# 2-byte in place of 4-byte TensorE transposes, no dummy matmuls among the first scale columns, and another place for the wait before the last store, in a transformer block

## The chip, the cores and the metric

The kernel runs on one core of a Trainium2 chip. The metric is the device time of one execution in microseconds (us), the median of the runs of a measurement. The core has a matrix engine (TensorE, PE in the profile, its weight loads PEld), VectorE (DVE), ScalarE (ACT) and GpSimd (POOL). SyncE (SP) issues most of the data transfers. All five work from queues of their own and meet through semaphores.

## What is computed

The block has two token sequences of 256 tokens, 1152 features, two heads of 576 and a hidden layer of 4608. All inputs are bf16.

```python
mod = (_silu(c) @ w_mod).reshape(B, 6, 1, D)
shift_a, scale_a, gate_a, shift_m, scale_m, gate_m = [mod[:, i] for i in range(6)]
h = _layernorm(x, axis=-1) * (1 + scale_a) + shift_a
qkv = (h @ wqkv).reshape(B, N, 3, H, Dh)
attn = _softmax(jnp.einsum('bqhd,bkhd->bhqk', q, k) * Dh ** (-0.5), axis=-1)
a = jnp.einsum('bhqk,bkhd->bqhd', attn, v).reshape(B, N, D) @ wo
x = x + gate_a * a
h2 = _layernorm(x, axis=-1) * (1 + scale_m) + shift_m
m = _gelu(h2 @ w_fc1) @ w_fc2
return x + gate_m * m
```

## The kernel before

**Tiles.** The 512 tokens stand in four tiles of 128 partitions (tile t, sequence b = t // 2). Matmuls contract over features, so activations must stand with features on the partitions: 1152 features are 9 slices of 128 (index kt). LayerNorm 1, the softmax and LayerNorm 2 have tokens on the partitions, and their outputs are transposed by TensorE into PSUM, from where VectorE and ScalarE copy them out. PSUM has 8 banks of 2 KB per partition.

**Order of work.** The program is recorded as units (`S.unit`, `S.op`). `Sched.schedule` is a planner: TensorE's and SP's units keep the order in which they are recorded, the other engines take the ready unit with the longest remaining chain, by costs written in the code (a transpose unit costs its count times `c_mm(128)`). For the first part of VectorE's and ScalarE's work the order is written out by hand in `S.first` (lines 935 to 941). `Sched.emit` turns the dependences into semaphore waits. The dependences in PSUM are by whole banks (lines 257 to 279): a read of a bank by ScalarE waits for earlier recorded reads of the same bank by VectorE, and the other way round, and a TensorE write waits for all readers of the bank before it.

**4-byte transposes.** `tr4` (line 703) looks at 256 neighbouring bf16 values of a token as 128 words of 4 bytes and transposes the words against a 4-byte identity (`IDENT4W`, made by GpSimd, line 735). The result has two features in one word: on partition p the features 2p and 2p+1 of the group lie side by side. A LayerNorm tile needs one 2-byte transpose (`tr`, line 707; slice 0) and four of `tr4` (slices 1 to 8, in pairs). So whatever reads the result steps by two elements, and the weight rows that meet it are loaded in the same paired order (`pair`, `wqkv_row`, `fcols`, `wqkv_h`, `wfc1_h`). The softmax transposes have two `tr4` for each of four (sequence, head) pairs, and their pairs are keys, so the value matmuls take every second token (`v0`, line 985).

**The first part.** Fourteen dummy matmuls (`warm(14, "b")`) stand ahead of the first transposes. Then come transposes xnT_1, xnT_0 and the first scale columns (`mod_kt`, units sca_0 to sca_8, 5 matmuls of 2 columns each) in three groups of three kt, as their weights arrive. Two dummy matmuls of 512 columns stand after sca_5 (`warm(2, "c")`), two after sca_8 (`warm(2, "d")`). Then `sc1a`, the scaled slices `hk(kt, b)` for kt 0 to 4 out of PSUM (kt 2 and 4 of sequence 0 and kt 2 of sequence 1 by ScalarE), and the key matmuls, slice by slice; xnT_2 stands after kt 1 and xnT_3 after kt 2. `XB` (line 780) has the three banks of each sequence: slice 0 in the third, slices 1 to 4 in the first, 5 to 8 in the second. `xn_T_copy` copies 5 to 8 out in one ScalarE instruction.

**LayerNorm 2.** `wo_tile(t)` has three chunks of nine matmuls, each followed by VectorE (line 1065) and GpSimd (line 1066), then the statistics and `xn2_t` (ScalarE, line 1071). `xn2_T(t)` has the transposes: slice 0 and slices 5 to 8 in bank 6, 1 to 4 in bank 7. VectorE copies out slices 0 to 3 for tiles 0 and 1 and 0 to 5 for tiles 2 and 3 (line 1088), ScalarE the rest (line 1091). xn2T_0 stands ahead of `wo_tile(3)`, xn2T_1 ahead of its third chunk, xn2T_2 after fc1 tile 3, xn2T_3 after fc1 tile 5 (F0 is 8).

**The end.** The second MLP matmul stores 14 pieces; token tile 3 ends in pieces of 384, 384, 224, 96 and 64 columns. Each piece is multiplied and added on VectorE (lines 1181, 1182) and stored by SP. Before SP issues the last store, lines 469 to 471 wait for the end of all the others.

Of the kernel before, what the change touches and what calls it, by code (L numbers as in the profile page):

```python
# [171 lines left out]
class Sched:  # L172
# [225 lines left out]
    def emit(self, nc, block, sems, dma_sems):  # L398
# [67 lines left out]
        def run_engine(e, eng_handle):  # L466
            for u in order[e]:
                for ins in u.instrs:
                    if ins is last_out:
                        for o in outs[:-1]:  # L470
                            eng_handle.wait_ge(dma_sems[o.dma_sem], o.dma_val)
# [10 lines left out]
            if e == "sp":  # L482
                eng_handle.wait_ge(dma_sems[last_out.dma_sem], last_out.dma_val)
# [11 lines left out]
F32R = mybir.dt.float32r  # L495
# [48 lines left out]
def build_kernel(nc, x, c, wqkv, wo, w_mod, w_fc1, w_fc2, out):  # L544
# [5 lines left out]
    with (  # L550
# [4 lines left out]
        arena_off = nc.sbuf_base - ARENA_BYTES  # L555
        words = nc.alloc_sbuf_tensor_at("words", [P, ARENA_BYTES // 4], F32R, offset=arena_off)

        def sb(off, nbytes, dt=BF16):
            assert off % 4 == 0 and off + nbytes <= ARENA_BYTES, (off, nbytes)
            v = arena[:, off // 2:(off + nbytes) // 2]  # L560
            if dt != BF16:
                v = v.bitcast(dt)
            return v
# [65 lines left out]
        o_id4 = misc(512)  # L629
        IDENT4 = sb(o_id4, 512)  # L630
        IDENT4W = nc.alloc_sbuf_tensor_at("ident4", [P, P], F32R, offset=arena_off + o_id4)[:, :]
# [26 lines left out]
        wqkv_h = wqkv[P:D, :].rearrange("(g p i) f -> p g i f", p=P, i=2)  # L658
        wmod_v = w_mod.rearrange("(k p) f -> p k f", p=P)
        wo_v = wo.rearrange("(k p) f -> p k f", p=P)  # L660
        wfc1_h = w_fc1[P:D, :].rearrange("(g p i) f -> p g i f", p=P, i=2)
# [6 lines left out]

        def pair(kt):
            return (kt - 1) // 2, (kt - 1) % 2  # L670

        def wqkv_row(kt, c0):
            if kt == 0:
                return wqkv[0:P, c0:c0 + D]
            g, i = pair(kt)
            return wqkv_h[:, g, i, c0:c0 + D]

        def fcols(ft):
            if ft == 0:
                return slice(0, P)  # L680
            g, i = pair(ft)
            c0 = P + 256 * g + i
            return slice(c0, c0 + 255, 2)
# [19 lines left out]
        def tr4(o, i_):  # L703
            o4, w0 = o.bitcast(F32R), int(i_.offset) % (ARENA_BYTES // 2) // 2
            S.instr(lambda e: e.transpose(o4, words[:, w0:w0 + P], IDENT4W), reads=[i_, IDENT4], writes=[o])  # L705

# [7 lines left out]
        for (ka, kb) in ((0, KC), (KC, KT)):  # L714
# [4 lines left out]
            for kt in range(ka, kb):  # L719
                dma(WK[:, kt, :], wqkv_row(kt, D), P * D * 2, "ld_wk%d" % kt, run=2304)  # L720
# [3 lines left out]
        def wfc1_load(q):  # L724
            w = WFC1[q % 4]
            dma(w[:, 0, :], w_fc1[0:P, q * 512:(q + 1) * 512], P * 512 * 2, "ld_wfc1_%d_0" % q, run=1024)
            for i in range(2):
                dma(w[:, 1 + i:KT:2, :], wfc1_h[:, :, i, q * 512:(q + 1) * 512], 4 * P * 512 * 2, "ld_wfc1_%d_%d" % (q, 1 + i), run=1024)
# [6 lines left out]
        pool(300, lambda e: e.tensor_copy(IDENT4W, IDENT), [IDENT], [IDENT4], "ident4")  # L735
# [46 lines left out]
        def xn_T(t):  # L782
            b = t // 2
            S.unit("pe", 5 * c_mm(128), "xnT_%d" % t)
            tr(ps16(XB[b][2], (t % 2) * 128, 128), XN[:, t, 0:P], IDENT)
            for g in range(4):
                tr4(ps32(XB[b][g // 2], (g % 2) * 256 + (t % 2) * 128, 128), XN[:, t, P + 256 * g:P + 256 * (g + 1)])

        def xn_src(b, kt):
            if kt == 0:  # L790
                return ps16(XB[b][2], 0, 256)
            g, i = pair(kt)
            return ps16(XB[b][g // 2], (g % 2) * 512, 512).rearrange("p (t i) -> p i t", i=2)[:, i, :]

        def xn_T_copy(b, eng):
            src = ps16(XB[b][1]).rearrange("p (g t i) -> p g i t", g=2, i=2)
            dst = HX[:, KC:KT, b * 256:(b + 1) * 256].rearrange("p (g i) t -> p g i t", i=2)
            copy_on(eng, dst, src, 4 * 256, True, "xnT_cp%d" % b)
# [6 lines left out]
        def mod_kt(W, kt, col0, name, fs=(0, 9)):  # L805
            S.unit("pe", (fs[1] - fs[0]) * 27.0, name)
            for f in range(*fs):
                mm(ps32(7, col0 + f * 2, 2), W[:, kt, fcols(f)], ST[:, kt:18:9], kt == 0 and f == fs[0], kt == KT - 1,
                   skip_group_check=True)
# [6 lines left out]
        def hk(kt, b, eng="dve"):  # L816
            dst, s1 = HK[:, kt, b * 256:(b + 1) * 256], SC1A[:, kt * 2 + b:kt * 2 + b + 1]
            src = xn_src(b, kt) if kt < KC else HX[:, kt, b * 256:(b + 1) * 256]
# [38 lines left out]
        warm(2, "c")  # L857
        for kt in range(6, 9):
            mod_kt(WSC, kt, 0, "sca_%d" % kt, (0, KC))
        warm(2, "d")  # L860
# [3 lines left out]
        xn_T_copy(0, "act")  # L864
        for kt in range(KC):
# [4 lines left out]
            if kt == 2:  # L870
                xn_T(3)
                xn_T_copy(1, "act")
# [11 lines left out]
        for kt in range(KT):  # L884
            dma(WQ[:, kt, :], wqkv_row(kt, 0), P * D * 2, "ld_wq%d" % kt, run=2304)
# [28 lines left out]
        dma(WV[:, 0, :], wqkv_row(0, 2 * D), P * D * 2, "ld_wv0", run=2304)  # L914
        for i in range(2):
            dma(WV[:, 1 + i:KT:2, :], wqkv_h[:, :, i, 2 * D:3 * D], 4 * P * D * 2, "ld_wv%d" % (1 + i), run=2304)
# [4 lines left out]
        for kt in range(KT):  # L921
            for b in range(2):
# [5 lines left out]
                else:  # L928
# [10 lines left out]
            "act": ["ld_c", "c_tanh", "sq_ln1_0", "sum_ln1_0", "sq_ln1_3", "sum_ln1_3", "xnT_cp0", "hk_2_0", "hk_4_0",  # L939
                    "hk_2_1", "xnT_cp1"],  # L940
# [28 lines left out]
        def pt_transposes(b, h):  # L969
            idx = b * 2 + h  # L970
            bank = s_bank[(b, h)]
            S.unit("pe", 2 * c_mm(128), "PT_%d_%d" % (b, h))
            for jq in range(2):
                tr4(ps32(bank, jq * 128, 128), PP[idx][:, jq, :])
# [263 lines left out]
```

## Time and profile before

| what | value |
|---|---|
| median of 3 runs | 250.79 us (250.44 to 250.94) |
| the profiled execution's own time | 250.94 us |
| its span in the profile | 249.1 us |
| TensorE matmul busy | 240.2 us |
| 4-byte transposes (L705) | 40, 6.0 us busy, median 252 ns |
| 128x128 2-byte transposes (L708) | 8, 1.8 us busy, mean 221 ns |
| VectorE reads of 128x128 slices from PSUM (L1088) | 20, 328 to 409 ns, median 402 ns |
| idle before 4-byte and 128x128 2-byte transposes | 0.4 and 1.7 us |
| share of DMA engines, first half of the span | 0.9 and more |

Busy time is the sum of stretches in which an engine had an instruction in it. Matmuls overlap: one of 384 columns has a duration of 326 ns, and a row of them advances by 162.5 ns each, so what a matmul costs is read from the distance of starts or ends. "Idle before" is the time in which an engine had nothing, with the instruction that ended it; its releaser is inferred, and an engine can also be held from an instruction in the middle of a group. `L701` is the helper of all matmuls, `L705` of the 4-byte transposes, `L708` of the others, and `L666` of all transfers.

### The profile page before, as it was taken

The numbers are of one execution on the slowest core, as the hardware profiler recorded it, in microseconds if no ns is written. First come the engines' busy times: TensorE is split into PE (matmuls) and PEld (weight loads), VectorE is DVE, ScalarE is ACT, GpSimd is POOL, SyncE is SP. The second block draws the span as 40 slices with busy tenths as digits, with TensorE's granted clock in tenths as the row PEclk, the third lists the DMA queues.
The fourth block names the chain that finished last, engine by engine and source line by source line (L and its number), as shares of the span: only waits on it lengthen the run. The fifth ranks groups of instructions, "written<-read, shape, count | busy, mean of one in ns | idle before, by whom it ended". The sixth has DMA issues, their size and how long they took to land.

```text
span 249.1 us, 4079 instructions
## 1 busy us (share of the span) xinstructions
PE 240.2 (96%) x1777; PEld 148.3 (60%) x1787; DVE 71.5 (29%) x179; ACT 63.8 (26%) x127; POOL 19.9 (8%) x34
## 2 busy tenths in 40 slices
PE   6899999999999999899999999999999999999995
PEld 2489954557656756588644444444565665665674
DVE  3753440456422679842000000000011222211112
ACT  4730340344301404785323322233000000000000
POOL 1300000000023166500000000000000000000000
PEclk9999999999999999999999999999999999999999
DMA  6999999999999999999955560000000000000000
GB/s 238 362 379 389 391 343 414 419 429 420 404 379 328 309 366 391 393 345 323 356 175 168 168 189 0 3 0 0 0 18 16 16 16 18 16 16 19 31 17 20
DMA packets 27965, 51.60 MB, mean 207 GB/s; under 512 B 1831, under 2 KB 15911, under 8 KB 26795
## 3 DMA queue, kind: packets, MB, share of 16 engines
q1 hardware_dynamic: 27536, 50.14, 55.7%
q0 software_dynamic: 384, 1.19, 1.6%
q8 instruction: 14, 0.23, 0.4%
q14 instruction: 4, 0.03, 0.0%
q10 hardware_dynamic: 27, 0.00, 0.0%
HBM read 50.14 MB, written 1.19 MB: 206 GB/s over the span
## 4 chain that ended last, share of the span: by engine, by line
PE 91%; DMA 3%; DVE 2%; ACT 1%; SPq 1%; issue 1%
PE psum L701 90%; DMA arena<-in_w_mod_dram 3%; ACT arena L1091 1%; PE psum L705 1%; SPq L666 1%; DVE arena L1065 1%; DVE arena L1088 0%; PE psum L708 0%; DVE arena L753 0%; DVE arena L1070 0%; ACT arena L1101 0%; DVE arena L822 0%; DVE arena L909 0%; DVE arena L1181 0%; DVE arena L1182 0%
## 5 line engine op out<-in xcount | busy, mean ns | idle before, releaser
L701 PE MATMUL psum<-arena 128*128 128x384 bf16 (+7 forms) x1710 | 237.1, 305 | 2.9 <-POOL arena L731 1.4
L701 PEld LDWEIGHTS psum<-arena 128*128 128x128 bf16 (+1 forms) x1720 | 143.2, 97 | 91.7 <-issue 2.6
L1181 DVE TENSOR_TENSOR arena<-psum,arena 128x384 f32<-128x384 f32 (+3 forms) x14 | 7.0, 501 | 118.8 <-PE psum L701 118.8
L1101 ACT ACTIVATE arena<-psum 128x512 bf16<-128x512 f32 (+1 forms) x44 | 22.5, 522 | 42.6 <-PE psum L701 42.6
L696 ACT ACTIVATE arena<-psum 128x512 bf16<-128x512 f32 (+6 forms) x27 | 15.3, 582 | 35.5 <-PE psum L701 33.4
L698 DVE CAST arena<-psum 128x512 bf16<-128x512 f32 (+4 forms) x23 | 14.0, 621 | 32.0 <-PE psum L701 31.9
L1066 POOL TENSOR_TENSOR arena<-arena 128x384 f32<-128x384 f32 x12 | 10.9, 912 | 11.7 <-DVE arena L1065 9.5
L753 DVE BATCH_NORM_STATS2 arena<-arena 128x6 f32<-128x384 f32 (+1 forms) x18 | 9.6, 550 | 1.6 <-POOL arena L1066 0.9
L1071 ACT ACTIVATE arena<-arena 128x1152 bf16<-128x1152 f32 x4 | 5.4, 1350 | 9.5 <-DVE arena L1070 9.5
L1065 DVE TENSOR_TENSOR arena<-psum,arena 128x384 f32<-128x384 f32 x12 | 6.6, 548 | 3.2 <-PE psum L701 3.0
L1091 ACT ACTIVATE arena<-psum,arena 128x128 bf16<-128x128 bf16 x16 | 6.1, 461 | 4.8 <-PE psum L701 4.8
L1088 DVE TENSOR_SCALAR arena<-psum,arena 128x128 bf16<-128x128 bf16 x20 | 6.5, 390 | 2.5 <-PE psum L705 2.5
L1182 DVE TENSOR_TENSOR arena<-arena 128x384 bf16<-128x384 f32 (+3 forms) x14 | 7.0, 502 | 0.5
L705 PE MATMUL psum<-ident,words 128*128 128x128 f32 x40 | 6.0, 261 | 0.4 <-DVE arena L909 0.4
L666 POOL DMA_DIRECT2D dit_scratch<-arena x2 | 1.3, 632 | 61.4 <-DVE arena L698 61.4
L963 ACT ACTIVATE arena<-psum,arena 128x256 bf16<-128x256 f32 x8 | 3.7, 470 | 6.9 <-PE psum L701 5.4
L705 PEld LDWEIGHTS psum<-ident,words 128*128 128x128 f32 x40 | 4.4, 141 | 0.9 <-DVE arena L909 0.5
L708 PE MATMUL psum<-arena 2*128 2x2 bf16 (+2 forms) x27 | 2.5, 179 | 2.5 <-DVE arena L1065 0.9
L708 PEld LDWEIGHTS psum<-arena 2*128 2x128 bf16 (+2 forms) x27 | 1.3, 93 | 5.0 <-DMA arena<-in_c_dram 1.7
L757 POOL TENSOR_TENSOR arena<-arena 128x1 f32<-128x1 f32 x6 | 3.3, 554 | 8.4 <-DVE arena L756 8.4
L822 DVE TENSOR_SCALAR arena<-psum,arena 128x256 bf16<-128x256 bf16 x7 | 2.9, 443 | 2.4 <-PE psum L705 1.7
L926 ACT ACTIVATE arena<-arena 128x256 bf16<-128x256 bf16 x6 | 2.5, 497 | 4.3 <-DVE arena L920 4.3
(40 smaller groups left out, 36.9 us busy)
## 6 DMA issues: line engine op xcount, KB each, us to landing
arena<-in_w_mod_dram SPq DMA_DIRECT2D x3, 3456.0 KB, 23.8
arena<-in_w_fc_dram SPq DMA_DIRECT2D x4, 2592.0 KB, 19.7
arena<-in_w_fc_dram SPq DMA_DIRECT2D x18, 512.0 KB, 6.7
arena<-in_wqkv_dram SPq DMA_DIRECT2D x19, 288.0 KB, 9.0
arena<-in_w_mod_dram SPq DMA_DIRECT2D x3, 864.0 KB, 11.9
arena<-in_wo_dram SPq DMA_DIRECT2D x1, 2592.0 KB, 36.5
arena<-in_wqkv_dram SPq DMA_DIRECT2D x2, 1152.0 KB, 8.7
arena<-in_w_mod_dram SPq DMA_DIRECT2D x3, 480.0 KB, 7.4
```

The costliest lines, as they stand in the source:

```text
L696: act(c_act(n), lambda e: e.activation(out=dst, in_=src, func=ACTF.Copy), [src], [dst], name)
L698: dve(c_dve_psum16(n) if psum16 else c_dve_psum32(n), lambda e: e.tensor_copy(dst, src), [src], [dst], name)
L701: S.instr(lambda e: e.matmul(o, lhsT=l, rhs=r, start=st, stop=sp, **kw), reads=[l, r], writes=[o])
L705: S.instr(lambda e: e.transpose(o4, words[:, w0:w0 + P], IDENT4W), reads=[i_, IDENT4], writes=[o])
L753: dve(550, lambda e, s=s, o=o: e.bn_stats(out=o, in_=s), [s], [o], "bn_%s_%d" % (tag, ci))
L1065: dve(550, lambda e, o=o, ga=ga, x1c=x1c: e.tensor_tensor(out=x1c, in0=o, in1=ga, op=ALU.mult), [o, ga], [x1c], "wo_t1_%d_%d" % (t, ci))
L1066: S.op("pool", 930, lambda e, xs=xs, x1c=x1c: e.tensor_tensor(out=x1c, in0=x1c, in1=xs, op=ALU.add), reads=[x1c, xs], writes=[x1c], name=" ...
L1088: dve(335, lambda e, o=o, dst=dst, s1=s1, s2=s2: e.tensor_scalar(out=dst, in0=o, scalar1=s1, scalar2=s2, op0=ALU.mult, op1=ALU.add), [o, s ...
L1091: act(440, lambda e, o=o, dst=dst, s1=s1, s2=s2: e.activation(out=dst, in_=o, func=ACTF.Identity, scale=s1, bias=s2), [o, s1, s2], [dst], ...
L1101: act(c_act(ntok), lambda e: e.activation(out=dst, in_=o, func=ACTF.Gelu_apprx_tanh), [o], [dst], "gelu_%d_%d" % (f, tok0))
L1181: dve(c_dve_psum32(w), lambda e, o=o, gm=gm, t1=t1: e.tensor_tensor(out=t1, in0=o, in1=gm, op=ALU.mult), [o, gm], [t1], "fc2_t1_%d_%d" % ( ...
L1182: dve(c_dve_32(w), lambda e, t1=t1, x1c=x1c, ost=ost: e.tensor_tensor(out=ost, in0=t1, in1=x1c, op=ALU.add), [t1, x1c], [ost], "fc2_out_%d ...
```

## The change

All 4-byte transposes become 2-byte ones, of 128 features each: nine in place of five for a LayerNorm tile, four in place of two for a softmax block. The paired order goes with them: weights are loaded in their natural row order, activations and PSUM slices are read without a step. The first MLP weights come in one transfer for each block of 512 columns in place of three, the value weights in one in place of three. Slices now lie in the banks in order: LayerNorm 1 has kt 0 to 3 in the first bank of `XB[b]`, 4 to 7 in the second and 8 in the third, and slices 5 to 8 are copied out in two instructions (8, then 5 to 7); LayerNorm 2 has kt 0 to 3 in bank 7 and 4 to 8 in bank 6. The planner's costs of the transpose units follow their counts. The dummies "c" and "d" are left out. SP waits for all stores but the last two before it issues the last one, and for the last but one afterwards.

```diff
                     if ins is last_out:
-                        for o in outs[:-1]:
+                        for o in outs[:-2]:
                             eng_handle.wait_ge(dma_sems[o.dma_sem], o.dma_val)
...
             if e == "sp":
+                for o in outs[-2:-1]:
+                    eng_handle.wait_ge(dma_sems[o.dma_sem], o.dma_val)
                 eng_handle.wait_ge(dma_sems[last_out.dma_sem], last_out.dma_val)
...
         def wfc1_load(q):
-            w = WFC1[q % 4]
-            dma(w[:, 0, :], w_fc1[0:P, q * 512:(q + 1) * 512], P * 512 * 2, "ld_wfc1_%d_0" % q, run=1024)
-            for i in range(2):
-                dma(w[:, 1 + i:KT:2, :], wfc1_h[:, :, i, q * 512:(q + 1) * 512], 4 * P * 512 * 2, "ld_wfc1_%d_%d" % (q, 1 + i), run=1024)
+            dma(WFC1[q % 4], wfc1_v[:, :, q * 512:(q + 1) * 512], D * 512 * 2, "ld_wfc1_%d" % q, run=1024)
...
-        pool(300, lambda e: e.tensor_copy(IDENT4W, IDENT), [IDENT], [IDENT4], "ident4")
...
         def xn_T(t):
             b = t // 2
-            S.unit("pe", 5 * c_mm(128), "xnT_%d" % t)
-            tr(ps16(XB[b][2], (t % 2) * 128, 128), XN[:, t, 0:P], IDENT)
-            for g in range(4):
-                tr4(ps32(XB[b][g // 2], (g % 2) * 256 + (t % 2) * 128, 128), XN[:, t, P + 256 * g:P + 256 * (g + 1)])
+            S.unit("pe", KT * c_mm(128), "xnT_%d" % t)
+            for kt in range(KT):
+                tr(ps16(XB[b][kt // 4], (kt % 4) * 256 + (t % 2) * 128, 128), XN[:, t, kt * 128:(kt + 1) * 128], IDENT)
...
-        def xn_T_copy(b, eng):
-            src = ps16(XB[b][1]).rearrange("p (g t i) -> p g i t", g=2, i=2)
-            dst = HX[:, KC:KT, b * 256:(b + 1) * 256].rearrange("p (g i) t -> p g i t", i=2)
-            copy_on(eng, dst, src, 4 * 256, True, "xnT_cp%d" % b)
+        def xn_T_copy(b, k0, k1, eng):
+            src = ps16(XB[b][k0 // 4], (k0 % 4) * 256, (k1 - k0) * 256).rearrange("p (k t) -> p k t", k=k1 - k0)
+            copy_on(eng, HX[:, k0:k1, b * 256:(b + 1) * 256], src, (k1 - k0) * 256, True, "xnT_cp%d_%d" % (b, k0))
...
-            src = xn_src(b, kt) if kt < KC else HX[:, kt, b * 256:(b + 1) * 256]
+            src = ps16(XB[b][kt // 4], (kt % 4) * 256, 256) if kt < KC else HX[:, kt, b * 256:(b + 1) * 256]
...
-        warm(2, "c")
         for kt in range(6, 9):
             mod_kt(WSC, kt, 0, "sca_%d" % kt, (0, KC))
-        warm(2, "d")
...
-        xn_T_copy(0, "act")
+        xn_T_copy(0, 8, 9, "act")
+        xn_T_copy(0, 5, 8, "act")
...
-            S.unit("pe", 2 * c_mm(128), "PT_%d_%d" % (b, h))
-            for jq in range(2):
-                tr4(ps32(bank, jq * 128, 128), PP[idx][:, jq, :])
+            S.unit("pe", 4 * c_mm(128), "PT_%d_%d" % (b, h))
+            for kjt in range(2):
+                for jq in range(2):
+                    tr(ps16(bank, kjt * 256 + jq * 128, 128), PP[idx][:, jq, kjt * 128:(kjt + 1) * 128], IDENT)
...
-            S.unit("pe", 5 * c_mm(128), "xn2T_%d" % t)
-            slot = [ps16(6, 512, 128)]
-            tr(slot[0], xn2[:, 0:P], IDENT)
-            for g in range(4):
-                bank, c0 = (7, g * 128) if g < 2 else (6, (g - 2) * 128)
-                tr4(ps32(bank, c0, 128), xn2[:, P + 256 * g:P + 256 * (g + 1)])
-                v = ps16(bank, 2 * c0, 256).rearrange("p (t i) -> p i t", i=2)
-                slot += [v[:, 0, :], v[:, 1, :]]
+            S.unit("pe", KT * c_mm(128), "xn2T_%d" % t)
+            slot = [ps16(7, kt * 128, 128) if kt < 4 else ps16(6, (kt - 4) * 128, 128) for kt in range(KT)]
+            for kt in range(KT):
+                tr(slot[kt], xn2[:, kt * 128:(kt + 1) * 128], IDENT)
```

## The prediction

> **What bounds the kernel.** I read the page first, its busy times and its chain of work.
>
> ```profile
> PE 240.2 (96%) x1777; PEld 148.3 (60%) x1787; DVE 71.5 (29%) x179; ACT 63.8 (26%) x127; POOL 19.9 (8%) x34
> ...
> PE 91%; DMA 3%; DVE 2%; ACT 1%; SPq 1%; issue 1%
> ```
>
> TensorE sets the time. A change counts if it adds matmul time, removes a place where TensorE stands still, or moves the tail after the last matmul. So next I took the timeline wherever the start of one TensorE instruction lags the previous by far more than its length. After the first weights arrive (12.4 us) there are only three such regions. The first is in LayerNorm 1, transposes of token tile 2 (xnT_2):
>
> ```profile
> 13.27 0.47 ACT L820 ACTIVATE arena<-psum,arena 128x256 bf16<-128x256 bf16 x1 [2.23 <-DVE arena L822]
> 13.77 0.48 DVE L822 TENSOR_SCALAR arena<-psum,arena 128x256 bf16<-128x256 bf16 x1
> 14.20 0.34 PE L705 MATMUL psum<-ident,words 128*128 128x128 f32 x2
> 14.29 0.47 ACT L820 ACTIVATE arena<-psum,arena 128x256 bf16<-128x256 bf16 x1 [0.55 <-DVE arena L822]
> 14.91 0.34 PE L705 MATMUL psum<-ident,words 128*128 128x128 f32 x2 [0.37 <-DVE arena L909]
> ```
>
> See the ladder: hk_2_0 (ACT), hk_3_0 (DVE), hk_4_0 (ACT) run one after the other because all read PSUM bank 4, and the kernel orders readers of one bank on different engines. The third and fourth 4-byte transposes write bank 4 and start when the ladder ends (14.29+0.47). The page names L909, which ends at 14.84, but bank 4 explains it too: both end within 0.1 us. L909 itself waits only for an earlier transpose of the same tile. TensorE loses 0.53 us: the second pair would have started near 14.38.
>
> The other regions are in LayerNorm 2:
>
> ```profile
> 100.23 1.14 ACT L1091 ACTIVATE arena<-psum,arena 128x128 bf16<-128x128 bf16 x3
> 101.51 0.22 PE L708 MATMUL psum<-arena 128*128 128x128 bf16 x1 [0.86 <-DVE arena L1065]
> 101.89 0.34 PE L701 MATMUL psum<-arena 128*128 128x384 bf16 x1
> ...
> 102.46 1.28 DVE L1088 TENSOR_SCALAR arena<-psum,arena 128x128 bf16<-128x128 bf16 x4
> 102.89 1.86 ACT L1091 ACTIVATE arena<-psum,arena 128x128 bf16<-128x128 bf16 x5 [1.52 <-PE psum L701]
> 104.45 0.28 PE L701 MATMUL psum<-arena 128*128 128x256 bf16 x1 [0.36 <-ACT arena L1091]
> ...
> 109.60 1.18 ACT L1091 ACTIVATE arena<-psum,arena 128x128 bf16<-128x128 bf16 x3
> 110.92 0.22 PE L708 MATMUL psum<-arena 128*128 128x128 bf16 x1 [0.44 <-ACT arena L1091]
> 111.30 0.28 PE L701 MATMUL psum<-arena 128*128 128x256 bf16 x1
> ```
>
> By starts TensorE loses 1.03 us before 101.51, 0.64 before 104.45, 0.60 before 110.92, each time until ACT's last copy out of banks 6 and 7. ACT starts late at 102.89 because bank 6 also holds slice 0, which DVE must read first (102.46+0.33).
>
> The tail:
>
> ```profile
> 246.55 0.22 DVE L1182 TENSOR_TENSOR arena<-arena 128x64 bf16<-128x64 f32 x1
> 247.27 0.33 SPq L666 DMA_DIRECT2D out_dram<-arena  x1
> ...
> SPq L471 <- DMA out_dram<-arena: 0.8, 2, 0.4
> ```
>
> The last store's data is ready at 246.77, its issue comes at 247.27, and what lies between is the wait of line 471 for the 24 KB store ahead (issued 245.64, 1.5 us to landing).
>
> **The parts.**
>
> *Price of a 2-byte transpose.* The trace has eight, none after another; by ends each advances TensorE by 55 to 57 ns. The last three fc2 pieces, 36 matmuls each with a new weight load, take 3.45, 1.53 and 1.23 us (VectorE starts 240.08, 243.53, 245.06, 246.29): 95.8, 42.5 and 34.2 ns for 224, 96 and 64 columns. The line through the first two gives 55.8 ns at 128. I take 56. Bounds: 42.5 (the 96-column row) and 86 (what a 4-byte transpose advances). A unit of 9 is then 0.50 us against 0.385 (15.97 to 16.36), **+0.12** (0 to +0.39). A softmax transpose is 4×56 = 0.22 against 0.14 (period 1.60 us less nine 384-column matmuls of 162.5 ns), **+0.085** (+0.03 to +0.2).
>
> The Trainium skill (TensorE: Matmul & The Clock Gate, section Back-to-back issue gap) speaks against the change: it has a sustained 81 ns per 128-column matmul with its weight load. By it a unit would cost +0.34 and a softmax transpose +0.18, at most 1.7 us more in all, and the sum would be 251.5. The rows at 96 and 224 columns do not show such a floor, so the sum does not use it.
>
> *LayerNorm 1.* xnT_1 and xnT_0 are longer by 0.12 each, hidden: TensorE waits for the third scale load until 11.05 anyway, and the 15 matmuls before are done at 10.36. Without that cover it would be 0.24. For xnT_2 the slices move: 0 to 3 in one bank, 4 to 7 in the next, 8 alone. Readers of bank 4 are now hk_0 to hk_3; hk_4_0 has bank 5, so ACT does it straight after hk_2_0. VectorE's reads become contiguous, which this trace prices: hk_0_1 is contiguous, hk_1_1 is strided.
>
> ```profile
> 16.55 0.35 DVE L822 TENSOR_SCALAR arena<-psum,arena 128x256 bf16<-128x256 bf16 x1 [1.71 <-PE psum L705]
> ...
> 16.82 0.48 DVE L822 TENSOR_SCALAR arena<-psum,arena 128x256 bf16<-128x256 bf16 x1
> ```
>
> So hk_1_0 ends 13.10, hk_2_0 13.61, hk_3_0 14.00, hk_4_0 14.08, all before TensorE arrives at 14.17: the 0.53 goes. xnT_2 and xnT_3 cost 0.24. Net **-0.29** (-0.53 to +0.25). Nothing is late next: the key weights of slice 3 landed at 14.05, the later scale weights at 18.19, and TensorE would want them near 16.1 and 19.5. ACT's evacuation in two copies instead of one (1.02 us at 10.01) has until 13.1.
>
> *Softmax.* 4×0.085 = **+0.34** (+0.1 to +0.8): TensorE is dense there. The strided operands of the value, scale and shift matmuls cost nothing today: N=2 matmuls with stride-2 weights advance at 27 ns.
>
> *LayerNorm 2, walked.* TensorE reaches xn2T_0 0.05 late (97.22) and leaves at 97.72. Bank 6 now holds slices 4 to 8, which for tiles 0 and 1 are all ACT's (for tiles 2 and 3 VectorE still has 4 and 5), and bank 7 slices 0 to 3, all VectorE's. So ACT starts near 98.02, not 98.28. I assume three of five copies (0.35 apart) before xn2_1 (1.34): the last ends near 101.0, and xn2T_1 does slices 0 to 3 before it and five after: the next matmul at 101.41 (before 101.89). ACT's five copies of tile 1 start at 101.65 and end 103.5; VectorE's four, 0.26 apart instead of 0.32, end 103.55; the first fc1 tile ends at 104.25 (105.0). Then ACT carries the chain: xn2_2 at 104.2 (104.62), bound by VectorE's statistics; table load 1.28; two gelus; xn2_3 at 107.4 (107.83); two gelus; three copies to 110.35; xn2T_3's last five transposes; next matmul at **110.75 against 111.30**: -0.55, the two earlier parts included. Bounds: -0.9 (all three stalls all but gone) and +0.7 (none goes, +0.05 and four units with little cover).
>
> *Planner.* The unit costs change, so orders on ACT and VectorE may move; that is the width of the last term.
>
> *Dummies.* The two before the third scale load lie in 10.36 to 11.10, the other two beside VectorE's 11.79 to 12.35, so taking them out is 0 on the path. They cover a clock, see below.
>
> *Loads.* First-layer MLP weights come in one transfer for three, value weights in one for three. SP has fewer issues and passes none; the first MLP weights landed at 78.8, wanted at 103. The third row load (landed 68.6, wanted at 70.2) has the least room, 1.6 us. GpSimd's widening of the identity (0.29 us at 1.42) goes too; GpSimd has nothing to do until 6.9. Cost 0.
>
> *Tail.* Issue at 246.80 instead of 247.27, same 1.4 us: **-0.46**. The 56 KB store (issued 244.38, 2.3 us) landed at 246.65, still waited for, only 0.12 earlier. Bounds -0.5 to 0. The wait moved to the end finds a landed store.
>
> **Sum.** -0.55-0.46 = -1.0. The profiled run took 250.94 (span 249.1 and 1.8 around it), so 249.9; it is 0.15 over the median of the three runs, so **249.8** by the median.
>
> **Rivals.**
>
> *The clock falls (slower).* Place: 12.41, the first K matmuls. The dummies at the start began 0.427 us apart until 6.31 and 0.215 after: the array starts at half speed and needs some 3 us of work. Without the four dummies (4×0.215) the 4.0 us from 8.39 to 12.41 hold 0.86 us less work and idle gaps of 0.6 to 0.9. If that drops it to half, a stretch like 3.36 to 6.31 loses half of 2.95: +1.5. -1.0+1.5 gives **251.3**, two stretches 252.8. Decides if a 256-column matmul after 12.41 advances at about 215 ns, not 109. Against: gaps of 0.36 and 0.47 changed nothing.
>
> The Trainium skill (the same page, Part 4: PE-mode transpose) says that transposes do not count as work for that clock, which favours this rival; its Part 1 puts the fall only after about 3.4 us of idling, which speaks against. No row here separates them; by the first it is 251.3, by the second 249.8.
>
> *The stalls stay (slower).* TensorE pays six exposed units and four softmax ones, 6×0.12+0.34 = +1.06, while ACT's or VectorE's order, not the banks, sets the waits. With the tail, +0.6: **251.4**. For it: ACT has xn2 and a table load in the way whatever the banks. Against: L1091 starting only after VectorE's first copy.
>
> *Half of it.* LayerNorm 2 gains nothing beyond its own cost, or the 56 KB store still holds the last one: -0.3 to -0.5, **250.4**.
>
> **Numbers.** Forecast 0.55 (249.4 to 250.2), half 0.18, stalls stay 0.17, clock 0.10. Range 249.2 to 251.4, into the slower cases. A measurement here tells 0.2% (0.5 us) from no change. Faster: 0.55 and a third of half, 0.61. Slower: 0.22, nearly all of two rivals. Same 0.17.
>
> **What would show it.** Second transposes of xnT_2 without a gap; ACT copying tile 1 before 102; the third-tile copies done before 110.5; last issue within 0.1 us of VectorE's end. Wrong, if transposes advance at 80 ns or more, if K matmuls start at 215 ns, or if ACT's order moves the copies behind more gelus.

## The result, and the profile after

| | before | after |
|---|---|---|
| median, four runs each | 250.69 us (250.44 to 250.94) | 248.91 us (248.69 to 249.44) |
| the profiled execution: time, span | 250.94, 249.1 | 248.90, 246.9 |

The ratio is 0.9932, 95% interval 0.9913 to 0.9951: 1.78 us faster, where 1.0 was forecast, and below the range. Twelve more executions of the same kernel (a_again below) show that these four are one of two groups: in 8 of the 12 the TensorE clock fell for some microseconds (the profile gives the clock that was granted, 1.0 being full speed) and the time was 250.2 to 252.0; by the median of those twelve the kernel is not told from the one before. So there are two questions: why an execution with full clock gains 1.8, and when the clock falls.

The page after, its busy times and the shares of its chain of work:

```profile
PE 240.9 (98%) x1814; PEld 149.5 (61%) x1823; DVE 69.9 (28%) x179; ACT 63.8 (26%) x129; POOL 19.6 (8%) x33
...
PE 93%; DMA 3%; ACT 1%; SPq 1%; issue 0%; DVE 0%
```

TensorE is busy 0.7 us longer (240.9 for 240.2), has 2.2 us less span, and VectorE's 2% of the chain are gone: time went out of TensorE's waits, not out of its work. Where, the two traces tell stretch by stretch. The borders are starts and ends of TensorE units, an end being that of the last matmul ahead.

| stretch | before | after | difference | forecast |
|---|---|---|---|---|
| span start to the third scale load's landing | 11.05 | 10.55 | -0.50 | 0 |
| from there to the first key matmul | 1.36 | 1.35 | -0.01 | 0 |
| to the first softmax transposes | 48.52 | 48.39 | -0.13 | -0.29 |
| the four softmax transposes | 4.94 | 5.28 | +0.34 | +0.34 |
| to xn2T_0 | 31.48 | 31.46 | -0.02 | 0 |
| LayerNorm 2, end of the matmul ahead of xn2T_0 to the end of xn2T_3 | 14.13 | 12.62 | -1.51 | -0.60 |
| to VectorE's last instruction | 135.31 | 135.30 | -0.01 | 0 |
| to the end of the span | 2.34 | 1.95 | -0.39 | -0.46 |

(The forecast of -0.55 for LayerNorm 2 was a landing point that included +0.05 from the earlier parts.) The first line varies from profile to profile: over all profiles below this load landed between 10.30 and 11.32, with 10.30 in a kernel that changes only the softmax, and at 10.48 and 10.81 in two profiles of kernels that differ by the dummies alone. So it is not counted as an effect of the change. The four terms of the change sum to -0.13 + 0.34 - 1.51 - 0.39 = -1.69, and the medians differ by 1.78.

The chain of waits after, around LayerNorm 1 (start, length, what):

```profile
2.70 7.85 DMA arena<-in_w_mod_dram
...
11.90 1.92 PE psum L680 x16
13.82 0.50 PE psum L683 x9
14.32 0.87 PE psum L680 x8
15.20 0.50 PE psum L683 x9
15.70 4.32 PE psum L680 x65
```

The nine transposes of xnT_2 now run through: 0.50 us, 56 ns each, as forecast, with no wait inside. (L683 is the transposes' helper now, L680 the matmuls'.) The chain shows TensorE without a break from 11.90 on, but a matmul group can hide a short wait of its weights. The timeline, a little later (start, busy, engine, line, operation, and in brackets the idle time before and what ended it):

```profile
16.82 1.08 ACT L675 ACTIVATE arena<-psum 128x256 bf16<-128x256 bf16 x2
16.96 0.35 DVE L785 TENSOR_SCALAR arena<-psum,arena 128x256 bf16<-128x256 bf16 x1 [0.61 <-ACT arena L783]
17.93 0.35 DVE L785 TENSOR_SCALAR arena<-psum,arena 128x256 bf16<-128x256 bf16 x1 [0.62 <-ACT arena L675]
18.34 0.22 PEld L680 LDWEIGHTS psum<-arena 128*128 128x128 bf16 x3 [0.24 <-DVE arena L785]
```

Here is a wait that the change made. Slices 4 and 5 to 7 of the second sequence lie in one bank now. ScalarE's copy of 5 to 7 (until 17.90) is recorded ahead of hk_4_1, so VectorE's hk_4_1 stands idle 0.62 us for it, and TensorE's weight loads wait 0.24 for hk_4_1. That takes back 0.13 of the gain.

The timeline of LayerNorm 2 after:

```profile
100.29 0.92 PE L683 MATMUL psum<-arena 128*128 128x128 bf16 x9
...
100.76 0.28 PEld L683 LDWEIGHTS psum<-arena 128*128 128x128 bf16 x5 [0.26 <-ACT arena L1049]
...
101.06 5.56 PE L680 MATMUL psum<-arena 128*128 128x384 bf16 x45
101.26 1.85 ACT L1049 ACTIVATE arena<-psum,arena 128x128 bf16<-128x128 bf16 x5 [0.55 <-PE psum L683]
101.26 1.10 DVE L1046 TENSOR_SCALAR arena<-psum,arena 128x128 bf16<-128x128 bf16 x4
...
102.98 1.36 ACT L1033 ACTIVATE arena<-arena 128x1152 bf16<-128x1152 f32 x1
...
107.15 1.60 DVE L1046 TENSOR_SCALAR arena<-psum,arena 128x128 bf16<-128x128 bf16 x6 [0.90 <-PE psum L683]
...
107.97 1.18 ACT L1049 ACTIVATE arena<-psum,arena 128x128 bf16<-128x128 bf16 x3
108.92 0.74 PE L683 MATMUL psum<-arena 128*128 128x128 bf16 x9
109.49 1.25 PE L680 MATMUL psum<-arena 128*128 128x256 bf16 x10
```

Of the three waits of before, the first is down to 0.26 (the weight loads of xn2T_1 stand for ScalarE's copy; from the end of the matmul ahead xn2T_1 takes 0.76 where nine need 0.50), the second is gone (45 matmuls in a row from 101.06), and so is the third but for 0.07 (xn2T_3: nine transposes in one group). xn2_2 (line 1033) starts at 102.98, forecast 104.2. ScalarE's copies of tile 2 end at 109.15, before TensorE wants the fifth slice of xn2T_3; before the change they ended at 110.78 and TensorE stood.

The four signs that the prediction asked for are all there: xnT_2 without a gap, tile 1's copies by ScalarE before 102 (101.26), the third tile's done before 110.5, and below, the last issue within 0.1 us of VectorE's end.

The tail, from the timeline:

```profile
244.72 0.23 DVE L1140 TENSOR_TENSOR arena<-arena 128x64 bf16<-128x64 f32 x1
...
245.04 0.33 SPq L661 DMA_DIRECT2D out_dram<-arena  x1
```

The last store is issued 0.09 us after its data, 0.50 before.

### The profile page after: what moved, and what is told of

It reads as the page before. It is cut to its first block, busy times and chain, and to the rows that moved or that the text cites. A ratio compares the mean times of both kernels' runs of the same rounds, so it can differ in the third digit from the quotient of the medians.

```text
span 246.9 us, 4129 instructions
## 1 busy us (share of the span) xinstructions
PE 240.9 (98%) x1814; PEld 149.5 (61%) x1823; DVE 69.9 (28%) x179; ACT 63.8 (26%) x129; POOL 19.6 (8%) x33
## 4 chain that ended last, share of the span: by engine, by line
PE 93%; DMA 3%; ACT 1%; SPq 1%; issue 0%; DVE 0%
PE psum L680 91%; DMA arena<-in_w_mod_dram 3%; PE psum L683 2%; ACT arena L1049 1%; SPq L661 1%; ACT arena L1033 1%; DVE arena L785 0%; DVE arena L1139 0%; DVE arena L1140 0%; DVE arena L776 0%
## 5 line engine op out<-in xcount | busy, mean ns | idle before, releaser
L680 PE MATMUL psum<-arena 128*128 128x384 bf16 (+7 forms) x1707 | 237.1, 305 | 3.3 <-POOL arena L703 1.4
L680 PEld LDWEIGHTS psum<-arena 128*128 128x128 bf16 (+1 forms) x1716 | 143.7, 97 | 92.0 <-issue 3.9
L675 ACT ACTIVATE arena<-psum 128x512 bf16<-128x512 f32 (+7 forms) x29 | 15.4, 553 | 36.2 <-PE psum L680 33.8
L683 PEld LDWEIGHTS psum<-arena 128*128 128x128 bf16 (+2 forms) x107 | 6.4, 97 | 2.6 <-DMA arena<-in_c_dram 0.8
L683 PE MATMUL psum<-arena 128*128 128x128 bf16 (+2 forms) x107 | 7.8, 209 | 0.1
L1046 DVE TENSOR_SCALAR arena<-psum,arena 128x128 bf16<-128x128 bf16 x20 | 5.5, 336 | 2.0 <-PE psum L683 1.8
L920 DVE TENSOR_REDUCE arena<-psum 128x2 f32<-128x512 f32 x4 | 2.8, 689 | 1.5 <-PE psum L680 1.5
L785 DVE TENSOR_SCALAR arena<-psum,arena 128x256 bf16<-128x256 bf16 x7 | 2.4, 349 | 2.7 <-PE psum L683 1.4
L928 DVE TENSOR_TENSOR arena<-arena 128x512 bf16<-128x512 bf16 x4 | 2.8, 688 | 0.1
```

The source lines that it names most:

```text
L675: act(c_act(n), lambda e: e.activation(out=dst, in_=src, func=ACTF.Copy), [src], [dst], name)
L680: S.instr(lambda e: e.matmul(o, lhsT=l, rhs=r, start=st, stop=sp, **kw), reads=[l, r], writes=[o])
L683: S.instr(lambda e: e.transpose(o, i_, idn), reads=[i_, idn], writes=[o])
```

## The experiments

Times are medians with their range, ratios are to the kernel before on the same chip, intervals are of 95%. All kernels compute the whole block. "Stretch" is the LayerNorm 2 line of the table; such stretches repeat to 0.02 us between kernels that share the code, so one profile settles a tenth (two cases of 0.15 are named below with their cause).

### LayerNorm 2: banks or orders

**e_ln2**: before, with the LayerNorm 2 part alone.

```diff
-            S.unit("pe", 5 * c_mm(128), "xn2T_%d" % t)
+            S.unit("pe", KT * c_mm(128), "xn2T_%d" % t)
+            slot = [ps16(7, kt * 128, 128) if kt < 4 else ps16(6, (kt - 4) * 128, 128) for kt in range(KT)]
+            for kt in range(KT):
+                tr(slot[kt], xn2[:, kt * 128:(kt + 1) * 128], IDENT)
```

> The kernel before with the transposes of LayerNorm 2 alone made 2-byte (and the first MLP weights in natural order); the planner plans anew. The stretch from the end of the matmul ahead of xn2T_0 to the end of xn2T_3 took 14.13 us before and 12.62 after the whole change. If the gain of that stretch belongs to this part alone: 12.6, total -1.5 us against before. If it needs the earlier start of the first stages or the other parts: 13.5, the -0.6 of the prediction's walk.

249.53 us (248.70 to 249.95, 7 runs), ratio 0.9941, 0.9921 to 0.9962. Stretch 12.62, as in the changed kernel: the whole -1.51 is this part's own.

**e_ln2_oldorder**: the same, with VectorE's and ScalarE's instructions held in the order that the planner had chosen before the change.

```diff
+        S.first["dve"] = DVE_ORDER_BEFORE
+        S.first["act"] = ACT_ORDER_BEFORE
         S.schedule()
```

> The same, but VectorE and ScalarE keep the order of instructions of the kernel before, written out by hand. Theory A (banks and the planner's new order share the gain): the walk of the prediction was right for the old order, so the stretch takes 13.4 to 13.6 us, 0.8 to 1.0 more than with the new order. Theory B (the separate banks and shorter VectorE reads alone): 12.6, the same as with the new order.

251.20 (250.81 to 251.66, 11 runs), ratio 1.0007, 0.9994 to 1.0020. Stretch 13.91, and the way from there to VectorE's last instruction is 0.27 longer: with the order held, nothing of the gain is left. Neither theory had this number. The timeline of its tile 2:

```profile
107.97 1.60 DVE L1082 TENSOR_SCALAR arena<-psum,arena 128x128 bf16<-128x128 bf16 x6 [1.01 <-PE psum L708]
...
109.67 1.16 ACT L1085 ACTIVATE arena<-psum,arena 128x128 bf16<-128x128 bf16 x3 [0.37 <-DVE arena L1082]
...
110.97 0.44 PE L708 MATMUL psum<-arena 128*128 128x128 bf16 x5 [0.85 <-ACT arena L1085]
```

ScalarE starts its three copies only when VectorE has done all six, because the last of the six is slice 4, which lies in ScalarE's bank; TensorE waits 0.85 us for ScalarE. So the held order is not a neutral one: it takes slices 0 and 5 first, the two that shared ScalarE's bank in the old layout, and in the new layout those are slices 4 and 5.

**e_neworder**: before, with the new order of the statistics and of the third GELU, on the old banks with the 4-byte transposes.

```diff
-wo_t1_3_1, veps_ln2_2, bn_ln2_3_0, h2T_1_0, h2T_1_1, h2T_1_2, h2T_1_3, wo_t1_3_2, nmr2_2
+wo_t1_3_1, veps_ln2_2, h2T_1_0, h2T_1_1, h2T_1_2, h2T_1_3, nmr2_2, wo_t1_3_2, bn_ln2_3_0
 ScalarE:
-xn2_3, gelu_2_0
+gelu_2_0, xn2_3
```

> The kernel before, 4-byte transposes kept, with only the new places of three instructions: VectorE does nmr2_2 ahead of wo_t1_3_2 and bn_ln2_3_0 after it, ScalarE does gelu_2 ahead of xn2_3. Theory A says that the order alone has little to give while ScalarE still starts late at tile 1: stretch 13.6 to 14.0 us (before 14.13). Theory C (the order is the whole of it, the banks nothing): 12.6 to 12.9. If the new order hurts the old layout: over 14.2.

250.67 (250.27 to 251.54, 11 runs), ratio 0.9986, 0.9968 to 1.0004. Stretch 13.77. Its timeline at the second wait:

```profile
102.23 1.30 DVE L1088 TENSOR_SCALAR arena<-psum,arena 128x128 bf16<-128x128 bf16 x4 [0.52 <-PE psum L705]
102.67 1.85 ACT L1091 ACTIVATE arena<-psum,arena 128x128 bf16<-128x128 bf16 x5 [1.17 <-DVE arena L1088]
...
104.23 0.11 PEld L701 LDWEIGHTS psum<-arena 128*128 128x128 bf16 x2 [0.40 <-ACT arena L1091]
```

ScalarE still waits for VectorE's first copy, the one that shares its bank. So neither the new banks with their transposes and unstepped reads (-0.22) nor these moves of order (-0.36) bring the gain; the new banks with all of the planner's moves bring -1.51.

**s_banks_first**, **s_banks_act**, **s_stats** split the orders, on the new banks. In all three the orders of before are held, but for these moves:

```diff
 s_banks_first, VectorE, tiles 2 and 3:
-h2T_2_0, h2T_2_5, h2T_2_1, h2T_2_2, h2T_2_3, h2T_2_4
+h2T_2_4, h2T_2_5, h2T_2_0, h2T_2_1, h2T_2_2, h2T_2_3
 s_banks_act, that and ScalarE:
-h2T_0_5, h2T_0_6, xn2_1, h2T_0_4, h2T_0_7
+h2T_0_4, h2T_0_5, h2T_0_6, xn2_1, h2T_0_7
-h2T_1_5, h2T_1_6, h2T_1_7, h2T_1_4
+h2T_1_4, h2T_1_5, h2T_1_6, h2T_1_7
-xn2_3, gelu_2_0
+gelu_2_0, xn2_3
 s_stats, VectorE, only the statistics:
-wo_t1_3_1, veps_ln2_2, bn_ln2_3_0, h2T_1_0, h2T_1_1, h2T_1_2, h2T_1_3, wo_t1_3_2, nmr2_2
+wo_t1_3_1, veps_ln2_2, h2T_1_0, h2T_1_1, h2T_1_2, h2T_1_3, nmr2_2, wo_t1_3_2, bn_ln2_3_0
```

> The LayerNorm 2 part alone with the orders of before held, except that VectorE copies slices 4 and 5 of token tiles 2 and 3 (the two of its six that share bank 6 with ScalarE's) first instead of fourth to sixth. LayerNorm 2 stretch (end of the matmul ahead of xn2T_0 to the end of xn2T_3): 13.91 with all old orders, 12.62 with all new ones. Theory A (the last stall is ScalarE waiting for VectorE's read of slice 4, the last of six): ScalarE starts its copies of tile 2 some 0.4 us sooner, xn2T_3's second half too, stretch near 13.5. Rival B (the whole gain is the order of the statistics): 13.9.

> As the one before, and ScalarE in its new order too (three instead of two copies of tile 0 ahead of xn2_1, the third GELU ahead of xn2_3); VectorE's statistics still in the old order. Theory A: the stall inside xn2T_1 shortens by 0.33 and the copies of tile 2 move up again, stretch 13.0 to 13.3; what is left to 12.62 belongs to the statistics. Rival B: 13.6 to 13.9, since xn2_2 and xn2_3 start as late as before.

> The LayerNorm 2 part alone with the orders of before held, except VectorE's statistics (the last step for tile 2 ahead of the third wo chunk of tile 3, the first statistics of tile 3 after it). Theory A (slice 4 last still holds ScalarE): xn2_2 starts 0.7 us sooner, but the stretch stays at 13.8 to 13.9. Rival B (the statistics are the gain): 12.6 to 12.9.

One execution each: 251.36, 250.67 and 251.50 us, all with a fallen clock early on, which the stretch, at 98 us, doesn't feel. Stretches 13.35, 13.30 and 13.91. Copying 4 and 5 first brings 0.56, and the 0.27 behind it. ScalarE's order adds only 0.05: it shortens xn2T_1 by 0.35, but the 45 matmuls after it take 5.73 in place of 5.39. The timeline of s_banks_act shows who has it:

```profile
102.20 0.56 DVE L750 BATCH_NORM_STATS2 arena<-arena 128x6 f32<-128x384 f32 x1 [0.41 <-POOL arena L1064]
102.67 1.08 DVE L1082 TENSOR_SCALAR arena<-psum,arena 128x128 bf16<-128x128 bf16 x4
103.31 0.10 PEld L701 LDWEIGHTS psum<-arena 128*128 128x128 bf16 x1 [0.16 <-DVE arena L1082]
```

VectorE first does a statistic of tile 3, for which it waits on GpSimd, and starts its copies of tile 1 at 102.67, some 0.8 us after they could (xn2T_1 ends at 101.86); TensorE's weight loads then wait for copy after copy. With the statistics moved behind, the rest goes: 13.30 to 12.62 (e_ln2 differs from s_banks_act in that move alone). Alone, it brings nothing beyond the banks' own 0.22 (13.91). The stretches are those of theory A, the first 0.15 lower than it said; xn2_2 in s_stats starts only 0.4 us sooner than in e_ln2_oldorder, not 0.7. The moves act in series: the statistics pay only once the other two waits are gone.

**a_oldorder**: the changed kernel with the old orders held.

```diff
+        S.first["dve"] = DVE_ORDER_BEFORE
+        S.first["act"] = ACT_ORDER_BEFORE
         S.schedule()
```

> The kernel after with VectorE and ScalarE held to the order of the kernel before. Theory A: the LayerNorm 2 stretch goes from 12.62 to 13.4 to 13.6 us and the total is 0.8 to 1.0 us over that of the kernel after, near 249.8, the predicted time. Theory B: no difference, 248.9.

Stretch 13.91 again, 13.4 to 13.6 expected. 252.61 (250.51 to 253.55, 12 runs), ratio 1.0043, 1.0018 to 1.0068; 8 of the 12 with a fallen clock; the four at full clock have a median of 250.81 where 249.8 was expected.

### LayerNorm 1, softmax and the last store, one by one

**e_ln1**: before, with the LayerNorm 1 part.

```diff
-            S.unit("pe", 5 * c_mm(128), "xnT_%d" % t)
+            S.unit("pe", KT * c_mm(128), "xnT_%d" % t)
+            for kt in range(KT):
+                tr(ps16(XB[b][kt // 4], (kt % 4) * 256 + (t % 2) * 128, 128), XN[:, t, kt * 128:(kt + 1) * 128], IDENT)
```

> The kernel before with the transposes of LayerNorm 1 alone made 2-byte (and weights of q, k, v in natural order). From the first K matmul to the first softmax transpose 48.52 us before and 48.39 after the change. Expected 48.4: the 0.53 of the stall in xnT_2 goes, two transposes cost 0.24, and a new stall of 0.13 at hk_4_1, whose bank the copy of slices 5 to 7 now reads too. Rival: the first stall stays, 48.8. Total -0.15 us plus whatever the arrival of the third scale load does.

First key matmul to softmax 48.38 for 48.52: -0.14. 250.62 (249.91 to 252.12, 12 runs), ratio 0.9989, 0.9971 to 1.0006, not told from no change by the times.

**e_pt**: before, with the softmax part.

```diff
-            S.unit("pe", 2 * c_mm(128), "PT_%d_%d" % (b, h))
+            S.unit("pe", 4 * c_mm(128), "PT_%d_%d" % (b, h))
```

> The kernel before with the softmax transposes alone made 2-byte. The stretch of four took 4.94 us before and 5.28 after: 5.28 expected, +0.34 us in all, slower than before. If a transpose hidden behind something else were the reason, 4.94 and 0.

Softmax stretch 5.28 for 4.94: +0.34, 0.22 us for four transposes. 251.35 (250.72 to 252.35, 12 runs), ratio 1.0012, 0.9999 to 1.0026.

**e_store**: before, with the moved wait.

```diff
-                        for o in outs[:-1]:
+                        for o in outs[:-2]:
```

> The kernel before with the change of the last wait alone. The last issue comes 0.1 us after VectorE's end in place of 0.50, and the span ends 1.95 us after VectorE's end in place of 2.34: -0.4 us in all. If two stores in flight hinder each other, the landing takes longer by as much and the gain is 0.

Issue 0.10 after the data, tail 1.99 for 2.34. 250.50 (249.91 to 251.95, 12 runs), ratio 0.9981, 0.9966 to 0.9996: -0.46 by the medians, -0.35 by the tail.

### The clock

**e_nodummy**: before, without the four dummies.

```diff
-        warm(2, "c")
...
-        warm(2, "d")
```

> The kernel before without the dummies c and d. Theory: they lie in waits, 0. The first K matmul starts 1.31 us after the third scale load's matmuls, 256-column matmuls advance by 109 ns. Rival: the array's clock falls, they advance at 215 ns for 3 us or so, +1.5 us. The start of the first scale matmuls was 0.5 us earlier in the profile of after: if leaving out the dummies causes that, the third load lands near 10.55, if it varies from run to run, anywhere from 10.5 to 11.1.

252.09 (250.52 to 252.55, 12 runs), ratio 1.0032, 1.0012 to 1.0052. In 9 of 12 executions the mean granted clock is 0.993 or less (median 252.16), in 3 it is 1.0 (250.65). The windows view of its profile (the stretch, then busy time of PE, PEld, DVE, ACT and POOL with instruction counts, granted clock, share of DMA engines, GB/s):

```profile
10.42:13.83 3.41, 1.79 (x27) 1.49 (x28) 2.11 (x8) 0.66 (x2) 1.06 (x2) 1.00 1.04 395
13.83:17.24 3.41, 3.41 (x22) 2.59 (x19) 0.83 (x3) 0.56 (x2) 0.00 (x0) 0.50 1.10 360
```

Half speed comes in one piece, 3.41 us long, and behind it the clock is full again. So one fall costs up to 1.7 us of TensorE's work (half of 3.41); between the groups' medians it is 1.5 here. One such piece in some 249 us makes a mean granted clock of 0.993.

**e_dummy**: the changed kernel with the four dummies put back (the two lines above).

> The kernel after with the four dummies put back. 0: the K matmuls start as long after the third scale load's matmuls (1.31 us) with them as without them, and the total is that of the kernel after. If the dummies delay the scale matmuls or the first K matmul, up to +0.3. If the arrival of the third scale load hangs on them, it lands near 11.05 again and the total is +0.5.

249.15 (248.95 to 249.34, 6 runs), ratio 0.9932, 0.9911 to 0.9953, no fall in six. Its stretches are the changed kernel's, but for 0.13 us between the key matmuls and the softmax (48.52, and 48.38 when measured again as a_dummy_again), a wait for a load that is shown under e_best3: the dummies cost nothing that repeats.

**a_again** (the changed kernel itself) and **a_dummy_again** (e_dummy once more), side by side on one chip, no edit.

> The changed kernel itself, once more, in twelve executions instead of four. Question: does the TensorE clock fall in part of its executions, as it did in 8 of 12 of the kernel with the old orders held and in 9 of 12 of the kernel that only lost the four dummies? Theory A (the clock falls whenever the four dummies are missing, and the four executions shown were lucky): about 8 of 12 with a mean granted clock of 0.993 or less, these near 250.5, the others near 248.9, median near 250.4. Rival B (the changed kernel's own timing before the K matmuls keeps the clock up): all at 0.998 or more, 248.6 to 249.5.

> The changed kernel with the four dummies put back among the scale columns, once more, on the same chip. Theory A (the dummies hold the clock): at most 2 of 12 executions with a granted clock of 0.993 or less, median near 249.1. Rival C (how often the clock falls belongs to the chip or the hour, not to the dummies): the same share as the changed kernel beside it.

| | full clock | fallen (0.993 or less) | all, ratio |
|---|---|---|---|
| a_again | 4 of 12, 248.44 to 248.78 | 8 of 12, 250.22 to 252.02 | 250.41, 0.9974 (0.9944 to 1.0005) |
| a_dummy_again | 10 of 12, 248.73 to 249.31 | 2 of 12, 250.74 and 250.98 | 249.12, 0.9939 (0.9915 to 0.9962) |
| kernel before beside them | 18 of 23, 250.02 to 250.97 | 5 of 23, 251.43 to 252.35 | 250.56 |

Theory A: the changed kernel's clock falls in two executions of three, +2.2 us between the two groups' medians (250.65 and 248.49), more than one fall can cost. One of the eight (252.02, clock 0.986) fits two falls; the rest is open. With that share four at full clock in a row, as the first measurement had, would be one chance in 81; whether something favoured them stays open. At full clock a_again is 0.57 us under a_dummy_again; its third scale load landed 0.33 us earlier in the profile, and the rest of that is open too (an execution whose loads come early may also be one that keeps its clock).

### Versions

**e_best**: before with the moved wait, LayerNorm 1 and 2, without the four dummies, softmax transposes left at 4 bytes.

```diff
 e_best, against the changed kernel:
-            S.unit("pe", 4 * c_mm(128), "PT_%d_%d" % (b, h))
+            S.unit("pe", 2 * c_mm(128), "PT_%d_%d" % (b, h))
```

> The kernel after with the softmax transposes as in the kernel before (4-byte, two for four). The stretch of the four softmax transposes takes 4.94 us in place of 5.28, all else as after: -0.34 us against after. If the rest of after needs the 2-byte softmax, no gain.

**e_best2**: the same, with the key slices of sequence 1 recorded ahead of the copy out of the same bank.

```diff
                 xn_T_copy(1, 8, 9, "act")
-                xn_T_copy(1, 5, 8, "act")
         for kt in range(KC):
             hk(kt, 1, "act" if kt == 2 else "dve")
+        xn_T_copy(1, 5, 8, "act")
```

> The same, and hk_4_1 is recorded ahead of the copy of slices 5 to 7 of sequence 1, so that VectorE's hk_4_1 no longer waits for ScalarE's copy of 0.81 us out of the same bank. From the first K matmul to the first softmax transpose 48.39 in after, expected 48.26: the stall of 0.13 goes. -0.13 against the run without it. If TensorE then waits for something else there, 0.

250.39 (248.46 to 251.83, 12 runs), ratio 0.9963, 0.9935 to 0.9992, and 250.06 (247.92 to 251.76, 12 runs), ratio 0.9943, 0.9917 to 0.9970. Each fell in 8 of 12. The profiled execution of e_best fell, that of e_best2 didn't, so their timelines show one group of matmuls at both speeds. First e_best, then e_best2:

```profile
12.28 3.38 PE L700 MATMUL psum<-arena 128*128 128x256 bf16 x16 [0.76 <-DVE arena L810]
```

```profile
12.32 1.92 PE L700 MATMUL psum<-arena 128*128 128x256 bf16 x16 [0.76 <-DVE arena L810]
```

This is the test that the prediction named: the first key matmuls at half pace. In e_best2 key matmuls to softmax take 48.25 for 48.39, so the wait behind ScalarE's copy was worth the 0.13. The softmax stretch is back at 4.94 in both.

**e_best3** is e_best2 with the four dummies, **e_best4** with eight.

```diff
+        warm(2, "c")
...
+        warm(2, "d")
 e_best4:
+        warm(4, "c")
...
+        warm(4, "d")
```

> The parts that gained (the moved wait of the last store, the LayerNorm 1 banks, LayerNorm 2 and its orders), the softmax transposes left 4-byte, the key slice of channel tile 4 of the second sequence ahead of the ScalarE copy out of the same bank, and the four dummies kept. By the sum of the measured parts: the changed kernel at full clock (248.9) minus 0.34 (softmax) minus 0.13 (stall behind the copy) = 248.4, and, if the dummies hold the clock, at most 2 of 12 executions above 249.5. If it is not the dummies, a spread from 248 to 252 as without them.

> As the one before, with eight dummies instead of four (four in each of the two places). If more work before the first K matmuls holds the clock better, no execution of 12 falls, at the price of the added matmuls: the two gaps are 0.5 to 0.9 us long and four dummies take 0.86, so +0.4 to +0.8 us, 248.8 to 249.2. If the gaps swallow them it is 248.4.

248.67 (248.43 to 248.98, 6 runs), ratio 0.9908, 0.9881 to 0.9936, and 248.61 (248.47 to 248.73, 6 runs), ratio 0.9906, 0.9879 to 0.9933. Neither fell, in six executions each; a rate like a_dummy_again's 2 in 12 would leave six without a fall about one time in three, so that they never fall is not shown. The eight cost nothing: the gaps hold them. These two beat the kernel before and the changed kernel, the latter not by their best execution but because they did not fall. In the profile of e_best3 the wait behind hk_4_1 is gone too, but the stretch is 48.40: after the 24th of the 36 matmuls of 2 columns for the scale of slices 5 to 8 TensorE stands until 19.46, 0.15 us more than usual, as it stands until 19.27, 0.13 more, in e_dummy and nowhere else. The 25th is the first that needs the third of those scale loads, and that load landed at 19.41 and at 19.22, each time 0.05 us ahead. In the other profiles it was there in time.

## Why the prediction was wrong

**The step that failed is "LayerNorm 2, walked"**: its term was -0.60 for the stretch and measured -1.51; the other three (LayerNorm 1, softmax, tail) together measured -0.18 against -0.41. Its mechanism (the banks let ScalarE and VectorE copy at the same time) was right, but the walk kept both engines' orders, apart from three copies in place of two ahead of xn2_1, and the sentence under "Planner" took a change of orders for a spread instead of working it out. With the orders really kept, the banks give 13.91 (e_ln2_oldorder), only -0.22, so the walk was also too hopeful by 0.4 on its own terms: it overlooked that, of VectorE's six copies of tiles 2 and 3, the one of slice 4 came last and held ScalarE's bank. The planner took slices 4 and 5 first, -0.56, gave ScalarE a new order, -0.05, and moved the statistics behind VectorE's copies of tile 1, -0.68 once the others were in. Why it took 4 and 5 first can be read from the code (it prefers the longest remaining chain, and the bank dependence hangs ScalarE's copies on slices 4 and 5); no run isolated the planner's reason.

**"Bounds -0.9 (all three stalls all but gone)"** was too narrow a floor. The three waits that the prediction itself counted by starts, 1.03, 0.64 and 0.60, sum to 2.27, and a floor has to allow for all of it less the longer units (4 x 0.12): -1.8. What is left of the waits (0.26 and 0.07) makes it -1.46, near the -1.51.

**LayerNorm 1**: the wait of 0.53 went and the two units cost 0.23 (0.50 for 0.385 each), as said; "Nothing is late next" failed by 0.13, the copy out of hk_4_1's bank (e_best2 takes it away).

**Price of a 2-byte transpose**: right. 56 ns each, nine in 0.50 us, four in 0.22, +0.34 for the softmax. The Trainium skill (TensorE: Matmul & The Clock Gate, section Back-to-back issue gap) would have had 81 ns; the rows of nine that run through do not show it.

**Tail**: -0.46 forecast, -0.39 measured. **Loads** and the time between the third scale load and the first key matmul: 0, as said.

**The clock** was a rival with a chance of 0.10. By "gaps of 0.36 and 0.47 changed nothing" it was put too low: it came in 8 of 16 executions of the changed kernel, cost 1.9 us between the groups' medians (248.74 and 250.64) where 1.5 was forecast, and then nearly all the gain is gone: over a_again's twelve the ratio is 0.9974, 0.9944 to 1.0005. That the four executions of the result were all at full clock was luck as far as these runs tell. "0 on the path. They cover a clock" was right in both halves; the weight was wrong. Over all kernels without the four dummies it fell in 41 of 64 executions, in the variants that keep them in 12 of 98, in the kernel before in 30 of 116. The rate isn't the dummies' alone: on one chip all four single executions (s_banks_first, s_banks_act, s_stats and the kernel before) fell with dummies in.

**"The stalls stay"** is what e_ln2_oldorder shows with the planner's new orders taken away, and a_oldorder, at full clock 250.81, is near the kernel before.

## What to carry to other kernels

Where a planner orders the engines, a changed bank or cost is two edits: work out the order it will choose, or read it off, before walking the timeline, and ask of each copy whose bank it holds when it comes last. A wait that hides behind another is worth nothing until the other goes, so effects that are small one by one can sum to more. Dummy work that costs nothing on the path may hold a clock whose fall one lucky measurement doesn't show: take a dozen executions and read the granted clock of each before it is left out.

## What was not expected of the hardware

In the six profiles that fell early, half speed was granted in one piece of 3.41 us, starting at a point that differs from run to run (11.24 to 13.83). Four of them have a second piece, behind the last matmul, and the two lie 69 or 70 times 3.413 us apart. The Trainium skill (TensorE: Matmul & The Clock Gate, Part 1, under What's actually happening) has the same length, a free-running window of 3413 ns. It has the clock fall after an idle window; here the window ahead of a fall was not idle: TensorE was busy in 1.79 of 3.41 us in e_nodummy above, and in e_pt in 3.02:

```profile
8.34:11.75 3.41, 3.02 (x58) 2.05 (x57) 2.86 (x10) 2.15 (x3) 1.09 (x3) 1.00 1.03 376
11.75:15.16 3.41, 3.41 (x18) 2.47 (x17) 1.70 (x4) 0.95 (x2) 0.00 (x0) 0.50 1.07 379
```

Busy time is a poor guide, since many of the matmuls in it move 2 columns. Counting the columns moved, in matmuls and transposes whose start lies in the window, orders the windows ahead of the key matmuls better: 1,238, 2,764, 2,876, 2,906, 3,034 and 3,102 columns ahead of the six falls. In the thirteen profiles without an early fall but with a piece behind the last matmul, windows placed in steps of 3.413 us back from that piece have 3,388 or more there, with one exception (2,886, in a_oldorder, where a dummy of 512 columns starts 0.07 us ahead of the window and runs into it).

The count is not the rule, though. It was made after the runs, and windows further on, full of matmuls of 2 columns, kept the clock with fewer: 2,722 from 29.82 in a_dummy_again and 2,978 from 30.29 in the kernel before. Slid over every position, the emptiest early window of e_best4 has 3,900 columns (no fall in 6), while a_again has one of fewer than 3,102 in about 60% of positions (8 falls of 12); the kernel before has one in as many and fell less often. What the clock counts stays open.

Transposes seem to count: the window from 7.47 in the changed kernel kept the clock with 3,410 columns, of which some 1,100 belong to matmuls, while the one in e_nodummy fell with 3,102 that are all of matmuls. The same page (Part 4: PE-mode transpose) says that a transpose doesn't count as busy in the same way; these two windows speak against it.
